# First MLP block split by step, first inverse in 16x16 blocks, and a new early order in a delta-rule attention and MLP kernel

## The chip, the cores and the metric

The kernel runs on one core of a Trainium2 chip. The metric is the device time of one execution in microseconds, shown as the median of several runs. Everything is float32, except that the MLP weights arrive as 8-byte floats and are converted on the chip.

## The reference

There are 4 batches, 8 heads, 768 tokens and 48 values per head. Attention is a delta rule whose state (48x48 per head and batch) is read and changed at every token; the outputs are laid side by side to rows of 384 and go through an MLP with a hard-swish.

```python
k_n = k / (np.linalg.norm(k, axis=-1, keepdims=True) + 1e-06)
for t in range(S):
    y[:, :, t] = einsum('bhd,bhde->bhe', q[:, :, t], state)
    v_old = einsum('bhde,bhd->bhe', state, k_n[:, :, t])
    state = state + beta[t] * outer(k_n[:, :, t], v[t] - v_old)
...
h = x @ w_in                        # (3072, 384) @ (384, 2048)
g = h * clip(h + 3, 0, 6) / 6
out = g @ w_out                     # (3072, 2048) @ (2048, 384)
```

## The kernel before

The 768 tokens are cut into 24 steps of 32 tokens; the four batches stand beside each other on the 128 partitions. Within a step the recurrence is solved by a triangular system: a strictly triangular 32x32 matrix per head and batch (the L part of the tile LB) is inverted, and the inverse X takes L's place. Two steps make an MLP block of 256 columns, so there are 12 blocks.

*Loads.* `load_k`, `load_q` and `load_v` bring one step each in four DMAs of 48 KB. `load_w` brings one of 16 weight pieces (8 of w_in, 8 of w_out, 768 KB each) as raw 8-byte words to a place that is free at the time. SP issues most of them; ACT issues every other early k step, one q step, beta and the first stores of L.

*Weights.* A piece is turned to float32 by `scales` on ACT, which makes the power of two from the exponent bits by five activations (L298), and by `convert` on DVE with three operations (L317, L322, L327), the last of which needs the scale.

*Steps.* `norms` makes the inverse lengths of k for a group of steps (group 0: steps 0 and 1; then groups of four). `prep` multiplies them onto k (kb, POOL L383), makes a mask times beta (mb, L391), transposes kb and qb on PE (pt, L409) with a copy to KQ on ACT (L412), multiplies them (sc, L425), masks the result into LB (DVE L434), makes beta times kb (bkb, L438), and stores L to DRAM for the later groups (L450).

*Inverses.* For steps 0 and 1 `product` inverts by six matrix products on PE (pi, L485), each between DVE transposes and additions; the result is written at L543. For a group of four steps `inverse` loads all 128 triangles of the group, one to a partition, and eliminates with 60 DVE operations (L566 and L571); the result goes through DRAM (L576) back into LB (L584).

*Chain.* `chain` is the recurrence of a step: state times k and q (ks, L622), R (L635), X times R (pz, L643) copied to Z on ACT, the update of the state (su, L710, and L726), the output (py, L643), and the transposed output xT (yt, L699, L700). It needs the state of the step before.

*MLP.* `up` works through the 16 chunks of a block: three matmuls into ph (L760), a ReLU to t on ACT (L765), and the product g on DVE (L772), which is held back in `pending`. It starts when both steps of the block have their xT. `down` multiplies g by w_out (po, L795). From block 2 on, `down_by_seven` does that with seven products of quarters (L856) and sums on DVE (L842).

*Order.* Each engine works in the order in which the program issues. Up to step 5 of the chain that order is a written list of words, `ORDER`, one per piece of work: p, h, i, n, x with a step or group, and a, c, q, v, w, u, g for scales, conversions, loads, MLP chunks and held-back products. After that a loop with a fixed plan of 15 places per step mixes the chain of step t, the prep of a later step, the inverse of the next group and one MLP chunk per place.

Of the kernel before, what the change touches and what calls it, by code (L numbers as in the profile page):

```python
# [22 lines left out]
n0*8 n1 p0 n1 p0 n1 p0 q*2 p0 q p1 q p1 n1 p0 p1 a n1 a*2 p0 q*2 a*2 c a q p1 x0 n1*2 a n1*3 a  # L23
p2*2 x0 q c k2 p2 a p1 p3 x1 c p3*2 p2 a x1*2 p2 p4 p1 a*2 x1 k2*2 p3 p2 a*3 p3 k2 p5 x0 c*2
k2*3 p3 x0 c a*4 x0 k2 c*3 p4 p5 k2*2 x1 k2 x0 p4 c*2 p5 p4 p5 p4*2 p5 x1*2 k2 x0 p5 a x1 a i1 c
x0 x1 a x0 c x1 k2 x1 x0*2 k2 c i1 v k2 i1 x1 i1 x0 i1*2 a i1*2 x0 q i1*3 a i1 h0*2 i1*3 q i1*3
h0 i1*3 v i1 x1 i1 q i1 h0 i1*3 a i1*2 a h1 a*2 h1 i1*2 h0 i1 h1 q h1 i1 c i1 v h1*2 v i1 h1 k2
i1*5 v i1 v i1 v c w v i1 a c a*2 i1 a i1 c i1 v q i1 a v*2 i1 v a c i1*4 w i1*2 h1 n2 i1*4 a
i1*3 a i1 h2 i1*2 c a i1 a i1 n2 a c*2 u a g c n2 a c u a n2 g u n2*3 a n2 q c a g n2*2 a c a p6
h2 u h2 c p6 a w p6 u q*2 a v g q*2 a h2 p6 c q*2 v u p7 a q p6 a q p7 p6 v p8 c g q h2 v h2 a c  # L30
w a p7 a k3 h3 u k3 p8 u a h2*2 k3 c g k3 g c h3 c h3 p8 a u k3 a k3 p7 u g q p8 u q w k3 p7 h3
a p9 p8 c a p9 k4 g p9 k4 p7 a*2 g u k3 k4 c k4 h3 a h3 p9 c w k3 k4 k3 a p9 g*2 h3 a c h4 k4 k3
u a h3 c g k4 h4 k3 c w u p8 k3*2 g k3 h4 k3 q a n3 a c n3 c a n3 u q u g u h4 a g p9 a c k4 h4
c a n3 a u a w k4 i2 w*2 a*2 u n3 a h4 v h5 h4 c a u c g n3 c n3*2 g v*2 u h4 n3 u v n3 u c p10
q a*2 q g k4 v q i2 p11 k4 u k4*4 p10 i2*2 q*2 i2*2 k4 u v i2*2 h5 v g h5 i2 a i2 q i2 p10 u h5
u v i2*2 q u i2*2 c i2 p10 g u i2 p10 i2*4 p11 p10 h5*2 q u q h5 p11 g u p11 i2 u i2*2 p12 i2 g
i2*2 p11*2 u i2*2 u i2*3 g i2 u*2 g i2 u*2 g u g u*2 g u i2*6 u*4 h5
# [4 lines left out]
def kernel(  # L42
# [90 lines left out]
    def load_k(t, eng=nc.sync):  # L133

        g, i = group(t)
        if i == 0:
            needs(*(("kb", first(g - 2) + j) for j in range(size(g - 2) if g >= 2 else 0)))
            kfs[g] = stage.tile([P, GS, H, D], FP32, name="kf", bufs=2)
        for b in range(B):
            eng.dma_start(out=kfs[g][rows(b), i], in_=tokens(k, b, t))  # L140
            if b == B - 1:
                past.add(("k", t))
            yield

    def load_q(t, eng=nc.sync):
        if t < N:
            if t >= NQB:
                needs(("qT", t - NQB))
            for b in range(B):
# [30 lines left out]
    for t in kbufs + qbufs + bkbufs:  # L180
        nc.vector.memset(t[:, :, D:DP], 0.0)

# [5 lines left out]
    for j, value in enumerate((1.0, -1.0)):  # L188
# [10 lines left out]
    nc.vector.tensor_reduce(  # L199
        out=eye[:], in_=ident[:].rearrange("p (b c) -> p c b", b=B), axis=AX.X, op=ALU.add  # L200
    )
    blocks = const.tile([P, C // G], FP32, name="blocks")
    nc.vector.tensor_reduce(
        out=blocks[:], in_=eye[:].rearrange("p (n c) -> p n c", c=G), axis=AX.X, op=ALU.add
    )

    parity = const.tile([P, 2, 2], FP32, name="parity")
    nc.vector.memset(parity[:], 0.0)
    for b in range(B):
        for j, value in enumerate((-1.0, 1.0)):  # L210
            nc.vector.memset(parity[rows(b), b % 2, j : j + 1], value)

    beta_tok = persist.tile([P, N, C], FP32, name="beta_tok")
    nc.vector.transpose(out=beta_tok[:].rearrange("p n h -> p (n h)"), in_=beta_hm)

    state = persist.tile([128, B, NP, D], FP32, name="state")
    nc.vector.memset(state[:], 0.0)
# [11 lines left out]
    for i, value in enumerate((1152 - 7.5 / 16, -1600.0, -448.0, -704.0, 704.0 * 128, 1e-30)):  # L229
        nc.vector.memset(places[:, i : i + 1], value)  # L230
    powers = (
        (ACTF.Relu, 1.0 / 16), (ACTF.Abs, 1.0), (ACTF.Relu, 1.0), (ACTF.Abs, 1.0),
        (ACTF.Relu, -128.0),
    )
    WP, WF = 256, 2
# [9 lines left out]
    raws, parts = {}, {}  # L245


    NR = 4
    ds = [0]
    assert WP * NKT == WF * DM and NR * 2 <= NWI <= 2 * NR and NR * 2 * WF * DM <= NFC * DM  # L250

    def load_w(i, pool=stage):
        if i >= NW:
            return
        dst, src = weights[i]
        if i >= NWI:
            needs(("w", i - NWI + NR - 2 if i < NWI + 2 else i - 2))
        if src.dtype == FP32:
            nc.sync.dma_start(out=dst, in_=src)
            return  # L260
        if NR <= i < NWI:
            n = (i - NR) * 2 * WF
            raw = w_out[:, n : n + 2 * WF, :].rearrange("p f m -> p (f m)").bitcast(U32)
            raws[i] = raw.rearrange("p (s f z) -> p s f z", s=dst.shape[1], z=2)
        else:
            shape = [128, dst.shape[1], dst.shape[2], 2]
            if pool is stage:
                raw = spare[:, ds[0] % 2].bitcast(U32)
                raws[i] = raw.rearrange("p (s f z) -> p s f z", s=shape[1], z=2)
                ds[0] += 1  # L270
            else:
                raws[i] = pool.tile(shape, U32, name="d")[:]
# [15 lines left out]
    def scales():  # L288

        for i in range(NW):  # L290
# [6 lines left out]
            for n, (func, scale) in enumerate(powers):  # L297
# [3 lines left out]
                )  # L301
                if n == len(powers) - 1:
# [3 lines left out]
    def convert():  # L306

        for i in range(NW):
# [803 lines left out]
```

## Time and profile before

| | |
|---|---|
| median of 3 runs | 726.7 us (723.8 to 729.11) |
| span of the profiled execution | 725.1 us |
| busy: PE, DVE, ACT, POOL | 656.7, 454.9, 247.3, 89.5 us |
| first ph matmul of block 0 | 87.60 us |
| first po matmul of block 0 | 148.14 us |
| last matmul ends | 721.3 us |

A busy engine is one with an instruction at work. PE shows every float32 matmul as two records. TensorE's granted clock is shown beside the busy shares. An idle time is named after what ended it.

### The profile page before, as it was taken

How to read it: one execution, taken by the hardware profiler on the slowest of the kernel's cores; microseconds unless marked ns; L12 is line 12 of the kernel's file. 1: busy time of each engine (PE TensorE's matmuls, PEld its weight loads, DVE VectorE, ACT ScalarE, POOL GpSimd, SP SyncE). 2: the span in 40 equal slices, each digit the busy share in tenths (PEclk: the TensorE clock that was granted, in tenths of full speed). 3: DMA queues.
4: the chain of work that ended last, by engine and by line, in shares of the span. 5: the costliest groups of instructions: out<-in, count | busy, mean ns of one | idle time of the engine just before them, and what ended most of it. 6: DMA issues, size and time to landing. Idle time of an engine off the chain costs nothing.

```text
span 725.1 us, 25019 instructions
## 1 busy us (share of the span) xinstructions
PE 656.7 (91%) x10984; PEld 571.9 (79%) x10984; DVE 454.9 (63%) x1209; ACT 247.3 (34%) x467; POOL 89.5 (12%) x128
## 2 busy tenths in 40 slices
PE   0666839798979999999999999999999999999997
PEld 0455627666756789889889899898898898989997
DVE  6556996488583379665489464598444894533343
ACT  1763688593130331331322322322313213222130
POOL 3640024004031101041110031000000000000000
PEclk9966569899999999999999999999999999999999
DMA  7954437472042312421410411212302001000000
GB/s 135 298 119 89 112 91 176 90 183 37 8 96 48 75 32 42 90 36 26 96 32 15 98 33 31 52 21 60 53 2 50 13 16 39 2 24 1 23 1 22
DMA packets 135853, 44.72 MB, mean 62 GB/s; under 512 B 126112, under 2 KB 129184, under 8 KB 135744
## 3 DMA queue, kind: packets, MB, share of 16 engines
q1 hardware_dynamic: 126832, 40.99, 25.4%
q10 hardware_dynamic: 8912, 2.13, 1.5%
q8 instruction: 86, 1.41, 0.8%
q14 instruction: 23, 0.19, 0.1%
HBM read 32.60 MB, written 10.49 MB: 59 GB/s over the span
## 4 chain that ended last, share of the span: by engine, by line
PE 78%; issue 7%; DVE 5%; DMA 4%; POOL 2%; ACT 2%; SPq 1%; POOLq 0%; DVEq 0%
PE ph L760 31%; PE po L856 26%; PE po L795 3%; PE pz L643 3%; PE ks L622 3%; PE su L710 3%; PE py L643 3%; PE pt L409 3%; PE sc L425 2%; DMA kf<-in_k_dram 2%; DMA spare<-in_moe_w_in_dram 1%; PE pi L485 1%; ACT spare L298 1%; DMA vf<-in_v_dram 1%; PE yt L699 1%
## 5 line engine op out<-in xcount | busy, mean ns | idle before, releaser
L760 PE MATMUL ph<-xT,w_in 128*128 128x256 f32 x1152 | 269.6, 386 | 2.6 <-issue 2.3
L760 PEld LDWEIGHTS ph<-xT,w_in 128*128 128x128 f32 x1152 | 216.4, 193 | 34.7 <-issue 3.0
L765 ACT ACTIVATE t<-ph,halves 128x256 f32<-128x256 f32 x192 | 90.8, 474 | 207.3 <-PE ph L760 204.6
L772 DVE SCALAR_TENSOR_TENSOR g<-t,ph 128x256 f32<-128x256 f32 x192 | 79.8, 418 | 120.5 <-ACT t L765 120.3
L856 PE MATMUL po<-w_out,g 128*128 128x192 f32 x640 | 111.9, 327 | 0.0
L856 PEld LDWEIGHTS po<-w_out,g 128*128 128x128 f32 x640 | 104.2, 190 | 0.5
L856 PE MATMUL po<-spare,g 128*128 128x192 f32 x480 | 87.2, 330 | 0.0
L856 PEld LDWEIGHTS po<-spare,g 128*128 128x128 f32 x480 | 78.0, 190 | 1.2
L298 ACT ACTIVATE spare<-spare,places 128x768 uint16<-128x768 uint16 (+1 forms) x74 | 69.2, 940 | 7.7 <-DVE w_in L327 3.3
L566 DVE TENSOR_TENSOR pr<-A 128x30 f32<-128x30 f32 (+19 forms) x180 | 62.8, 349 | 4.1
L571 DVE TENSOR_TENSOR A<-A,pr 128x30 f32<-128x30 f32 (+19 forms) x180 | 61.9, 344 | 4.1
L842 DVE TENSOR_TENSOR g<-g 128x256 f32<-128x256 f32 x160 | 60.4, 428 | 3.7 <-PE po L856 3.5
L409 PE MATMUL pt<-ident,kb 128*128 128x128 f32 x96 | 18.3, 326 | 32.8 <-POOL kb L383 32.8
L795 PE MATMUL po<-w_out,g 128*128 128x384 f32 x128 | 45.4, 494 | 0.0
L383 POOL TENSOR_TENSOR kb<-kf,inv 128x384 f32<-128x384 f32 x24 | 23.5, 979 | 176.0 <-DVE inv L369 73.0
L412 ACT ACTIVATE KQ<-pt 128x512 f32<-128x512 f32 x48 | 28.2, 594 | 47.4 <-PE pt L409 47.4
L409 PEld LDWEIGHTS pt<-ident,kb 128*128 128x128 f32 x96 | 13.8, 167 | 36.0 <-POOL kb L383 33.8
L863 ACT ACTIVATE o<-po 128x192 f32<-128x192 f32 x40 | 13.2, 331 | 82.8 <-PE po L856 79.7
L391 POOL TENSOR_TENSOR mb<-beta_tok,mask 128x256 f32<-128x256 f32 x48 | 33.8, 724 | 56.2 <-DVE LB L434 56.2
L726 DVE TENSOR_TENSOR state<-state,su 128x384 f32<-128x384 f32 x46 | 23.3, 548 | 22.2 <-PE su L710 22.2
L795 PEld LDWEIGHTS po<-w_out,g 128*128 128x128 f32 x128 | 23.5, 192 | 12.9 <-issue 0.5
L635 DVE SCALAR_TENSOR_TENSOR R<-ks,parity,vf 128x192 f32<-128x192 f32 x46 | 16.9, 410 | 26.3 <-PE ks L622 26.2
(97 smaller groups left out, 581.5 us busy)
## 6 DMA issues: line engine op xcount, KB each, us to landing
spare<-in_moe_w_out_dram SPq DMA_DIRECT2D x8, 768.0 KB, 5.4
vf<-in_v_dram SPq DMA_DIRECT2D x96, 48.0 KB, 2.6
qb<-in_q_dram SPq DMA_DIRECT2D x92, 48.0 KB, 2.4
out_dram<-o SPq DMA_DIRECT2D x92, 48.0 KB, 1.6
kf<-in_k_dram SPq DMA_DIRECT2D x84, 48.0 KB, 2.8
w_out<-in_moe_w_in_dram SPq DMA_DIRECT2D x4, 768.0 KB, 9.6
LB<-x_dram SPq DMA_DIRECT2D x22, 128.0 KB, 3.1
x_dram<-A SPq DMA_DIRECT2D x5, 512.0 KB, 2.8
```

The lines of the kernel that those rows point to most:

```text
L298: nc.scalar.activation(out=z, in_=z if n else d.bitcast(I16)[:, :, :, 3], func=func, bias=places[:, n : n + 1], scale=scale,)
L391: nc.gpsimd.tensor_tensor(out=mb[:, e], in0=beta_tok[:, t, e:H:2].unsqueeze(2).unsqueeze(3).to_broadcast([P, NP, 2, C]), in1=mask2[:].unsq ...
L409: nc.tensor.transpose(pt[:, p, :], src[:, 2 * p : 2 * p + 2].rearrange("p e w -> p (e w)"), ident[:])
L566: nc.vector.tensor_tensor(out=pv, in0=A[:, j, j + 1 :].unsqueeze(1).to_broadcast([n, j, w]), in1=A[:, 0:j, j].unsqueeze(2).to_broadcast([n ...
L571: nc.vector.tensor_tensor(out=A[:, 0:j, j + 1 :], in0=A[:, 0:j, j + 1 :], in1=pv, op=ALU.subtract)
L643: nc.tensor.matmul(ps[rows(place(b)), D * h : D * h + D], lhsT=m(h)[rows(b)], rhs=z[rows(b), D * h : D * h + D], start=True, stop=True, sk ...
L760: nc.tensor.matmul(ph[:], lhsT=w_in[:, s, f * 128 : (f + 1) * 128], rhs=xT[:, s, :], start=(s == 0), stop=(s == NKT - 1),)
L765: nc.scalar.activation(out=t1[:], in_=ph[:], func=ACTF.Relu, bias=half, scale=1.0 / 6.0)
L772: nc.vector.scalar_tensor_tensor(out=g, in0=t1[:], scalar=1.0, in1=ph[:], op0=ALU.min, op1=ALU.mult)
L795: nc.tensor.matmul(pos[c][:], lhsT=gs[blk, f // 2][:, f % 2, c * P : (c + 1) * P], rhs=w_out[:, f, :], start=(f == 0), stop=(f == NFC - 1),)
L842: nc.vector.tensor_tensor(out=A(f, *out), in0=A(f, *a), in1=A(f, *b), op=op)
L856: nc.tensor.matmul(ps[n][:], lhsT=A(f - f % 2, *a)[:, f % 2], rhs=b[:, f], start=(f == 0), stop=(f == HF - 1),)
```

## The change

1. *First block by step.* `up(0)` becomes two generators, `up(0, 0)` and `up(0, 1)`, each for the 128 columns of one step, so the first needs the xT of step 0 alone. Each matmul, ReLU and product of block 0 is issued twice with half the columns. ReLUs (`relus`) and products (`pending`) are now both held back, and are words of their own.
2. *First group's inverse.* For group 1 `halves_of` eliminates only the two 16x16 blocks on the diagonal, both in one operation (28 operations instead of 60). `join` then makes the block between them, per step, with two products on PE, two DVE transposes, an addition and a copy on ACT.
3. *Powers of two* take four activations instead of five.
4. *Order.* `ORDER` is new and finer: loads, settings, pads, masks, stores of L, and the output half of a chain are words too, and a piece of work is cut at more places. All loads and stores of L and X are issued by SP. The weights' raw places change, and the temporary pool of the products is replaced by buffers of KQ. Norms of steps 0 and 1 are made one by one, those of group 1 by two; their squares are on ACT, and they take one operation less.

The loop after the list keeps its plan. The diff, cut to its core:

```diff
 ORDER = """
-n0*8 n1 p0 n1 p0 n1 p0 q*2 p0 q p1 q p1 n1 p0 p1 a n1 a*2 p0 q*2 a*2 c a q p1 x0 n1*2 a n1*3 a
...
+k*3 z*2 k w z k z q z*2 q*2 m0 n0 q n0 k n0 m1 k n0*2 k a n0 s k n0 c s k a w c a k p0 q n1 q s p0
+a q*2 p0*2 k c s k p0 s p0 k a q s q p0 a s q x0 m2 a q*2 a q s n1 x0 q s q c n2 b0 q n1 q c q k
...
     powers = (
-        (ACTF.Relu, 1.0 / 16), (ACTF.Abs, 1.0), (ACTF.Relu, 1.0), (ACTF.Abs, 1.0),
-        (ACTF.Relu, -128.0),
+        (ACTF.Relu, 1.0 / 16, 1152 - 7.5 / 16), (ACTF.Abs, 1.0, -1600.0), (ACTF.Abs, 1.0, -1152.0),
+        (ACTF.Relu, -128.0, 704.0 * 128),
     )
...
+    homes = [spare[:, i] for i in range(2)] + [
+        w_out[:, n : n + 2 * WF, :].rearrange("p f m -> p (f m)") for n in range(0, NFC, 2 * WF)
+    ]
+    for i, n in enumerate((0, 1, 2, 3, 4, 5, 0, 1, 3, 4, 5, 0, 1, 5, 0, 1)):
...
-            if g in (2, 3):
+            if g < 4:
                 nc.scalar.activation(out=sq[:], in_=kf[:, i0 + i], func=ACTF.Square)
...
+    def lower(t, dma=nc.sync):
...
+            dma.dma_start(
+                out=l_dram[g][i].rearrange("h p c -> p h c"),
+                in_=LBs[t][:].rearrange("p e a j w -> p (e a) j w")[:, :, 0, :],
+            )
...
+    def join(t):
...
+        nc.vector.transpose(out=T, in_=LT)
+        yield
+        ps = times("pi1", T, HC)
+        yield
+        nc.vector.tensor_tensor(
+            out=S[:, :, HC:C], in0=ps[:], in1=corner[:].unsqueeze(1).to_broadcast([P, H, HC]),
+            op=ALU.add,
+        )
+        nc.vector.transpose(
+            out=T2.rearrange("p h c -> p (h c)"), in_=S.rearrange("p h c -> p (h c)")
+        )
+        yield
+        ps = times("pi2", T2, C)
+        yield
+        nc.scalar.activation(out=LT[:, :, HC:C], in_=ps[:], func=ACTF.Copy)
...
+    def halves_of(g):
...
+        for j in range(1, HC - 1):
+            w = HC - 1 - j
+            nc.vector.tensor_tensor(
+                out=pv, in0=D2[:, :, j, j + 1 : HC].unsqueeze(2).to_broadcast([n, 2, j, w]),
+                in1=D2[:, :, 0:j, j].unsqueeze(3).to_broadcast([n, 2, j, w]), op=ALU.mult,
+            )
+            nc.vector.tensor_tensor(
+                out=D2[:, :, 0:j, j + 1 : HC], in0=D2[:, :, 0:j, j + 1 : HC], in1=pv,
+                op=ALU.subtract,
+            )
...
-    def up(blk):
+    def up(blk, half_of=None):
+        cols = slice(0, TB) if half_of is None else slice(half_of * P, half_of * P + P)
+        name = "u" if half_of is None else "ab"[half_of]
-        needs(*(("seam", blk * CB + i) for i in range(CB)))
+        needs(*(("seam", blk * CB + i) for i in range(CB) if half_of in (None, i)))
...
                 nc.tensor.matmul(
-                    ph[:], lhsT=w_in[:, s, f * 128 : (f + 1) * 128], rhs=xT[:, s, :],
+                    ph[:, cols], lhsT=w_in[:, s, f * 128 : (f + 1) * 128], rhs=xT[:, s, cols],
...
+        ua=up(0, 0), ub=up(0, 1), u=mlp_units(),
...
-            for t in range(LA):
-                drain(load_k(t, nc.scalar if t % 2 else nc.sync))
```

## The prediction

> **What bounds the kernel now.** I read the page's busy shares, then the slices, then busy time by stage, then the timeline at the borders between stages.
>
> ```profile
> PE 656.7 (91%) x10984; PEld 571.9 (79%) x10984; DVE 454.9 (63%) x1209; ACT 247.3 (34%) x467; POOL 89.5 (12%) x128
> ...
> PE   0666839798979999999999999999999999999997
> ...
> PEclk9966569899999999999999999999999999999999
> DMA  7954437472042312421410411212302001000000
> ```
>
> The 91% is an average over two regimes: about 12 slices (18.1 us each) with holes and a reduced clock, then 28 at 9. I therefore cut the span at three events: the first matmul of the first MLP block (ph, 87.6), the first of its down projection (po, 148.1), and the end of step 7's py (250.7). Columns: window, its length, busy us (instructions) of PE, PEld, DVE, ACT, POOL, then granted clock, DMA share, GB/s.
>
> ```profile
> 0.00:87.60 87.60, 47.55 (x1719) 40.18 (x1719) 59.48 (x156) 43.79 (x61) 24.55 (x46) 0.77 0.64 156
> 87.60:148.10 60.50, 43.07 (x906) 36.00 (x903) 43.28 (x96) 43.35 (x68) 13.53 (x16) 0.82 0.52 123
> 148.10:250.70 102.60, 95.59 (x1512) 68.42 (x1511) 65.60 (x157) 35.38 (x64) 21.91 (x28) 0.97 0.32 67
> 250.70:721.30 470.60, 470.51 (x6861) 427.30 (x6853) 286.17 (x802) 124.83 (x276) 29.54 (x39) 1.00 0.17 35
> ```
>
> From 250.7 on PE is idle for 0.1 of 470.6 us. What can be won lies before. The events that hold it there, in the timeline (start, length, engine, line, what; in brackets the idle time before):
>
> ```profile
> 8.89 4.76 ACTq L140 DMA_DIRECT2D kf<-in_k_dram  x8
> 9.11 0.55 DVE L351 TENSOR_REDUCE ss<-sq 128x8 f32<-128x384 f32 x1
> 13.70 0.31 ACT L355 ACTIVATE root<-ss,places 128x16 f32<-128x16 f32 x1 [11.39 <-DMA kf<-in_k_dram]
> ...
> 67.80 0.41 DVE L543 SCALAR_TENSOR_TENSOR LB<-VY,pi 128x256 f32<-128x256 f32 x1
> ...
> 96.54 0.35 SPq L576 DMA_DIRECT2D x_dram<-A  x1
> ...
> 106.25 1.11 PE L409 MATMUL pt<-ident,kb 128*128 128x128 f32 x4 [12.56 <-POOL kb L383]
> ```
>
> Four readings. The first square root could run at 9.7 (ss done) but stands behind ACT's own DMA issues until 13.7. The first step's inverse is ready only at 68.2. The first group's inverse ends at 96.5. PE then waits 12.6 us for a kb that needs norms queued on DVE in between.
>
> [...] clock 0.77 in the first window, and six ph records take 2.16 us at 108.0 against a pitch of 1.29 later. [...] 0 to 38 us is DMA-full (8 or 9 tenths, 130 to 180 GB/s with 48 KB loads, 350 to 400 with weights) with two issuers.
>
> **The change part by part.** I add up PE work at the pitch of the dense stretch (start to start): ph 128x256 matmul 0.43 us, po of 384 columns 0.645, of 192 columns 0.325, ks 1.08 per step, pz, py, sc 0.8, su 0.82, yt 0.33, four pt 0.46; products of the inverse (pi) 0.8, with two operands 1.1. Over the listed instructions this is 613.3 us before; 460.1 of it lies after 250.7 and took 470.6, a factor 1.023.
>
> New PE work: four joins of two pi each, 8 x 0.75 = 6.0; the first block in two halves, 96 matmuls of 128 columns instead of 48 of 256. The trace has none of this form. At half the columns it costs 0.215, at no gain from fewer columns 0.43 (+20.6 in all). I take 0.225, since four pt with a 128x128 weight load each keep 0.44 to 0.46 us, so weight loads do not bind at 0.11. That is +1.0. Total 620.3: +7.0. The part after 250.7 is the same work in both, so the question is when the changed kernel has done 620.3 - 460.1 = 160.2.
>
> *To the first ph.* Work 24.9 on PE (28.8 before; step 1's chain is no longer ahead of it). Three queues run beside it.
> - DMA: all loads now go out on SP. The last v load of step 0 stands behind some 58 loads of 48 KB (0.34 us each: 140 GB/s) and 8 weight pieces (2.0 us each: 385 GB/s), so 2 + 20 + 16 = 38, and 41 landed. It also stands behind the store of step 3's LB (about 37).
> - DVE: to the first state update 45.5 us (conversions 19.4: 8 pieces of 0.55 + 0.95 + 0.96 less the last step; the two products 10.8; LB 4.1; ss 3.8; norms 3.6; settings and state the rest). It starts at 0.9 and idles about 9.6 early, until the first sc: k0 at 4.9, root 8.9 (no DMA issue ahead), kb 11, KQ 13, LB 16.8. End 56; ks1 to 57.
> - ACT: to the first xT 35 power operations x 0.94 = 32.9 (with the old five per piece 41), KQ 12 x 0.595 = 7.1, squares 7 x 0.52 = 3.6, six small copies and Z, y, xT 3.0, roots 1.2: 47.8. From 4.9, with 3.2 waiting for the first ss and some 3 for weight piece 2 (issued 46th on SP): 59.
> So the first ph comes at 59 (87.6 before).
>
> *First half* (16 chunks, steps 1's chain between): PE 10.8 + 3.85 = 14.7. DVE: 26 paired inverse operations of 28 to 112 elements 6.9 (between 0.18 and 0.27 in rows of 30 and 108), 16 g of 128 columns x 0.30 (between 0.18 and 0.418), state, y 2.3: 14.1. ACT 16 x 0.36 + 6 x 0.94 + 0.5 = 11.9. PE and DVE nearly equal, each handing to the other through four banks[...]: 18, to 77. The old inverse was 60 operations (66.1 to 96.5); the new has 28 and ends here at about 75.
>
> *Second half and joins*: PE 10.8 + 3.0 + 3.5 = 17.3; DVE 21.1 (g 4.8, conversions 6.9, R and y of two steps 4.2, ss, state, four join operations); ACT 14. DVE binds, and the join of step 2 waits for the return of the inverse through DRAM (about 84): 23, to 100.
>
> *To work 160.2*: 103.2 left, x 1.023 = 105.6. ACT still owes 19 power operations (17.9 of 25 us beside 23 us of PE work), from which the first po pieces come; the same stretch before had 102.6 for 87.9 x 1.023 = 90, so 12.6 of stalls. I take 10: to 216.
>
> Sum: 216 stands against 250.7, so 725.1 - 34.7 = 690.4. The profiled 725.1 lies 1.6 below the median 726.7 (723.8 to 729.1), so I say 692.
>
> Costed at nothing: settings moved to DVE in pieces and pads on POOL (POOL has 56 us idle before mb); shorter norms (four small operations of 0.18 to 0.35 instead of five; off the path after the first); SP's 21 extra issues (452 for 431, after 60 us SP is the idlest queue); copies split from their matmuls, deferred evictions (ACT 34% busy); the order after 250.7, where blocks stand half a period differently against the steps (ks now at the end of up instead of inside down), hidden while DVE stays near its 61%; if not, half a us a block, 5 in all.
>
> **The rivals.**
> A, the stalls stay: the start comes at 59 but the rest keeps the 35.9 us that stretch lost before (250.7 - 87.6 - 124.3 x 1.023). For: DVE and ACT carry about the same work into a shorter time, and half-size evictions are two for one. Against: the inverse no longer fills DVE. 59 + 135.3 x 1.023 + 35.9 = 233.3, + 474.4 + 1.6 = 709.
> B, denser: first ph at 53 (weights land without waiting), 6 of stalls: 197.4 + 474.4 (250.7 to the end) = 671.8, so 673 against the runs.
> C, slower: SP is the only load queue, and in-order. The store of LB(3) stands before v of step 0, and w_out loads before k and v, each waiting for ACT and DVE readers. If one such reader is late because of data queued behind that wait, the start slides one for one. Slower by over 1% (734) needs work 160.2 done only after 258, 42 us later than I put it, that is v of step 0 landing after 83 instead of 41; at 90 the time is 741. Against: LB(3) needs only loads that stand ahead of it.
> D, nothing won: C with v near 75 (692 + 34 = 726), or A with halves bound by weight loads (709 + 19.6 = 729).
>
> **How the numbers follow.** Main case 0.57 (679 to 704); A 0.22 (704 to 717); B 0.13 (664 to 679); D 0.04; C 0.04. Leaving out the thin ends of B and A: 668 to 714. One per cent, 7.3 us, is about what a measurement here can tell from no change: faster 0.92, same 0.04, slower 0.04.
>
> **What would show it.** First LB of the product before 35 (67.8 before), first ph 55 to 62, end of the inverse 73 to 80, first po 97 to 105, step 7's chain no later than about 225, then PE idle near nothing for some 470 us. Wrong: ph matmuls of 128 columns at a pitch over 0.3; a PE hole over 5 us between 60 and 200; v of step 0 after 50; holes after 250 that the kernel before does not have.

## The result, and the profile after

The changed kernel takes 717.17 us (median of 4 runs, 716.01 to 720.65) beside 725.28 for the kernel before in the same session (723.80 to 729.11): ratio 0.9896, 95% interval 0.9853 to 0.9940. Timed a second time it gave 0.9892 (0.9860 to 0.9925). It is faster by about 8 us where 34 were predicted, and 717.2 lies above the predicted range. The profiled span fell from 725.1 to 714.6.

The page's busy shares, slices and the row of the instruction queue, of the changed kernel:

```profile
PE 657.3 (92%) x11592; PEld 576.5 (81%) x11592; DVE 437.9 (61%) x1187; ACT 241.2 (34%) x479; POOL 88.3 (12%) x145
...
PE   1566978999996999999999999999999999999997
...
PEclk9985898999997999999999999999999999999999
DMA  7677774143116112343014043012051020100000
...
q8 instruction: 91, 1.49, 0.9%
```

DMA is still at 6 or 7 tenths for the first 100 us. The last row will matter: 91 packets of 16 KB on the queue that the page calls "instruction", beside 2 x 11592 instructions of the PE (matmuls and weight loads), so 254.8 for each packet. The kernel before has 86 packets for 2 x 10984, 255.4 for each. Counted in blocks of 256 that is 90.6 and 85.8 blocks.

Busy time by stage, cut at the same events as before: first ph, first po, the point where 160.1 us of PE work are done (counted with the prediction's pitches, so that the same 460 us are left as after 250.7 before), end of the last matmul. Columns as in the prediction: window, length, busy us (instructions) of PE, PEld, DVE, ACT, POOL, clock, DMA share, GB/s.

```profile
0.00:74.95 74.95, 38.49 (x1460) 32.81 (x1460) 46.20 (x104) 44.86 (x67) 27.73 (x65) 0.83 0.74 178
74.95:118.49 43.54, 37.02 (x966) 34.86 (x964) 30.81 (x99) 28.08 (x58) 0.41 (x2) 0.90 0.65 137
118.49:240.10 121.61, 111.05 (x2017) 81.25 (x2013) 75.94 (x179) 43.62 (x79) 28.62 (x36) 0.96 0.33 65
240.10:710.80 470.70, 470.70 (x7160) 427.63 (x7158) 284.60 (x805) 124.68 (x278) 31.56 (x42) 1.00 0.19 37
```

The last stage is as predicted (470.7 for 470.6). The miss lies in the stages before it, against the prediction's own terms:

| stage | predicted | measured | difference |
|---|---|---|---|
| to the first ph | 59 | 74.95 | +16.0 |
| first ph to first po (18 + 23) | 41 | 43.54 | +2.5 |
| first po to work 160 | 116 | 121.61 | +5.6 |
| sum | 216 | 240.1 | +24.1 |

What filled them shows in the list of the PE's waits up to 125 us (line, releaser, us in total, times, longest):

```profile
PE sc L497 <- issue: 6.3, 3, 2.3
PE pi L547 <- issue: 6.1, 4, 3.4
...
PE pi L635 <- issue: 1.9, 1, 1.9
PE pi L635 <- DVE VY L645: 1.9, 1, 1.9
...
PE pz L797 <- issue: 1.5, 1, 1.5
...
PE py L797 <- issue: 1.2, 1, 1.2
```

"issue" means that the PE waited for nothing that the profile shows. There are 12.4 us of it ahead of the first ph and 20 in the whole execution; the kernel before has 5 and 9. In the timeline these stops have a pattern (start, length, engine, line, what; in brackets the idle time before):

```profile
34.95 0.31 PE L497 MATMUL sc<-KQ 64*32 64x64 f32 x7 [0.33 <-ACT KQ L484]
37.38 0.80 PE L497 MATMUL sc<-KQ 64*32 64x64 f32 x57 [2.12 <-issue]
...
39.56 0.79 PE L497 MATMUL sc<-KQ 64*32 64x64 f32 x57
42.62 0.31 PE L497 MATMUL sc<-KQ 64*32 64x64 f32 x7 [2.26 <-issue]
...
58.34 0.59 PE L547 MATMUL pi<-VY 32*32 32x32 f32 x27 [3.38 <-issue]
```

Stops fall into the middle of one step's 64 score records, two for each of its 32 matmuls (the first after 7 of them, the second after 57), where a wait for data would be odd; `shift` below tests that. From one stop to the next I counted 125 to 128 matmul records, or twice that; with their weight loads, 128 records are a block of 256 instructions. Ahead of each of these resumptions the trace has one 16 KB packet of the instruction queue, started 2.3 to 2.8 us before it. Below, a *crossing* is the moment when the PE goes from one block into the next, and a *stop* is an idle time named "issue" at a crossing.

### The profile page after: what moved, and what is told of

It is laid out like the page before. It is cut to its first block, busy times and chain, and to the rows that moved or that the text cites. A ratio compares the mean times of both kernels' runs of the same rounds, so it can differ in the third digit from the quotient of the medians.

```text
span 714.6 us, 26278 instructions
## 1 busy us (share of the span) xinstructions
PE 657.3 (92%) x11592; PEld 576.5 (81%) x11592; DVE 437.9 (61%) x1187; ACT 241.2 (34%) x479; POOL 88.3 (12%) x145
## 4 chain that ended last, share of the span: by engine, by line
PE 84%; issue 8%; DMA 3%; SPq 3%; DVE 1%; ACT 1%; POOL 0%; POOLq 0%; DVEq 0%; ACTq 0%
PE ph L945 36%; PE po L1051 26%; PE po L986 3%; PE ks L776 3%; PE pz L797 3%; PE pt L479 3%; PE su L891 2%; PE py L797 2%; PE sc L497 2%; SPq L148 2%; DMA spare<-in_moe_w_in_dram 1%; PE pi L547 1%; PE yt L840 1%; SPq L160 1%; DMA w_out<-in_moe_w_in_dram 1%
## 5 line engine op out<-in xcount | busy, mean ns | idle before, releaser
L945 PE MATMUL ph<-xT,w_in 128*128 128x256 f32 (+1 forms) x1248 | 272.8, 373 | 6.3 <-DVE g L957 5.7
L945 PEld LDWEIGHTS ph<-xT,w_in 128*128 128x128 f32 x1248 | 221.8, 195 | 35.7 <-DVE g L957 6.5
L954 ACT ACTIVATE t<-ph,halves 128x256 f32<-128x256 f32 (+1 forms) x208 | 94.5, 456 | 244.6 <-PE ph L945 240.1
L957 DVE SCALAR_TENSOR_TENSOR g<-t,ph 128x256 f32<-128x256 f32 (+1 forms) x208 | 82.1, 397 | 104.2 <-ACT t L954 103.6
L720 DVE TENSOR_TENSOR pr<-A 128x30 f32<-128x30 f32 (+19 forms) x150 | 51.7, 345 | 5.7 <-DMA A<-l_dram 2.5
L338 ACT ACTIVATE spare<-spare,places 128x768 uint16<-128x768 uint16 (+1 forms) x56 | 52.3, 940 | 0.9
L725 DVE TENSOR_TENSOR A<-A,pr 128x30 f32<-128x30 f32 (+19 forms) x150 | 50.1, 334 | 3.6
L789 DVE SCALAR_TENSOR_TENSOR y<-ks,parity,y 128x192 f32<-128x192 f32 x46 | 17.0, 413 | 31.1 <-ACT y L813 31.1
L497 PE MATMUL sc<-KQ 64*32 64x64 f32 x1536 | 21.8, 230 | 10.4 <-issue 9.1
L776 PEld LDWEIGHTS ks<-state,KQ 64*64 64x64 f32 x1472 | 24.7, 138 | 7.6 <-issue 5.5
```

What stands on the lines that cost most here:

```text
L338: nc.scalar.activation(out=z, in_=z if n else d.bitcast(I16)[:, :, :, 3], func=func, bias=places[:, n : n + 1], scale=scale,)
L497: nc.tensor.matmul(scv[rows(b), e, p], lhsT=kq[:, 3 if b % 2 else 0, :], rhs=kq[:, 3:1:-1, :] if b % 2 else kq[:, 0:2, :], start=True, sto ...
L720: nc.vector.tensor_tensor(out=pv, in0=A[:, j, j + 1 :].unsqueeze(1).to_broadcast([n, j, w]), in1=A[:, 0:j, j].unsqueeze(2).to_broadcast([n ...
L725: nc.vector.tensor_tensor(out=A[:, 0:j, j + 1 :], in0=A[:, 0:j, j + 1 :], in1=pv, op=ALU.subtract)
L776: nc.tensor.matmul(ph[y][c, e, D * p : D * p + D], lhsT=KQ[r, p * B // 2 + b // 2, 2 * y : 2 * y + 2, :].rearrange("k y c -> k (y c)"), rh ...
L945: nc.tensor.matmul(ph[:, cols], lhsT=w_in[:, s, f * 128 : (f + 1) * 128], rhs=xT[:, s, cols], start=(s == 0), stop=(s == NKT - 1),)
```

## The experiments

Theory "fetch": streams of tiny matmuls use up blocks of instructions faster than these arrive. Its rivals: SP, held by the weight pieces, brings data late; or DVE and ACT, working through the written order, set the pace. Six kernels ran in one execution each: `shift`, `calm`, and the four that leave out part of the work (`thin`, `thin_trip`, `w_third`, `all_three`).

**Is it the block, or these matmuls?** `shift` moves every later PE instruction by 64 records:

```diff
-        for p in range(NP):
+        for p in [*range(NP)] * (2 if t == 0 else 1):
```

> The changed kernel with the 32 score matmuls of step 0 written twice over (the second writes the same values), so that all later instructions of the PE stand 64 instructions further on in its program. Fetch theory: the PE's idle stretches that the trace calls issue sit at instruction-block boundaries, every 256 PE instructions (128 matmuls with their weight loads), so counted in the program as it was they move 32 matmuls earlier, while the count of matmuls before each stays a multiple of 128 plus the same remainder: the first six stay at the same remainder, at other matmuls. If instead those stretches are waits of these particular matmuls for data or a semaphore that the trace doesn't show, each stays at its old matmul, 32 records later in the count. The time: within 4 us of the changed kernel either way.

The stops stayed at the count and left the matmuls. Matmul records issued at each stop of over 0.25 us ahead of the first ph:

```
changed kernel  475  601  726  980 1108 1236 1363
shift           475  601  728  980 1108 1236 1364 1491
```

In the timeline of `shift` the first stop is now inside a product of step 0, the second among the transposes:

```profile
34.74 0.26 PE L547 MATMUL pi<-VY 32*32 32x32 f32 x7
36.48 0.69 PE L547 MATMUL pi<-VY 32*32 32x32 f32 x57 [1.48 <-issue]
...
38.38 0.27 PE L479 MATMUL pt<-ident,kb 128*128 128x128 f32 x1
42.70 1.65 PE L479 MATMUL pt<-ident,kb 128*128 128x128 f32 x7 [4.05 <-issue]
```

So they are block ends, and no waits of these matmuls for data. (The one execution took 713.3 us; `shift64` below is the same program, timed.)

**Does it need a full DMA?** `calm` writes step 14's scores nine times over, at 282 us:

```diff
-        for p in range(NP):
+        for p in [*range(NP)] * (9 if t == 14 else 1):
```

> The changed kernel with the score matmuls of step 14 (at 282 us, where the DMA engines are about three tenths busy) written nine times over instead of once: 512 more matmul records, four blocks of 256 PE instructions, same values, same output. It measures how fast the PE can be fed with tiny matmuls when DMA is calm. Fetch with a floor of its own: the stream runs at its own pitch of 1.6 to 2.2 us per 128 records only for the first block, then stands at each block's end; a block lasts 3.5 to 3.9 us, the gaps are 1.3 to 2.2 us each, and the 512 records take 13 to 15.5 us. If only a full DMA makes the fetch late: no gap over 0.3 us and 6.5 to 9 us in all.

The PE's timeline there:

```profile
283.52 1.20 PE L497 MATMUL sc<-KQ 64*32 64x64 f32 x101
286.36 1.47 PE L497 MATMUL sc<-KQ 64*32 64x64 f32 x128 [1.63 <-issue]
290.09 1.92 PE L497 MATMUL sc<-KQ 64*32 64x64 f32 x128 [2.26 <-issue]
294.09 2.04 PE L497 MATMUL sc<-KQ 64*32 64x64 f32 x128 [2.08 <-issue]
297.82 1.57 PE L497 MATMUL sc<-KQ 64*32 64x64 f32 x91 [1.69 <-issue]
```

128 records need 1.5 to 2.0 us (1.5 at a granted clock of 1.00, 1.9 to 2.0 at 0.50 to 0.55), and a block comes only every 3.73, 4.00 and 3.73. After each of the first three resumptions the next packet of the instruction queue started 1.1 us later, and each packet started 2.4 to 2.9 us ahead of the resumption that it led to, while the DMA engines went from 0.51 busy to 0.02. So a full DMA is not needed for the stops: about 3.7 us per block remain with DMA nearly idle. The shortest time from one stop to the next in any of the runs is 3.5 us (`w_third`).

**Fewer instructions.** `thin` halves the matmuls of the first two steps' products:

```diff
-            for h in range(H):
+            for h in range(0, H, 2):
...
-                        ps[rows(b), 0:n, w], lhsT=T[rows(b), w], rhs=rhs[rows(b), :, w],
+                        ps[rows(b), 0:n, ww], lhsT=T[rows(b), w], rhs=rhs[rows(b), :, ww],
```

> The changed kernel with half the matmuls in the products that invert the first two steps: 16 of twice the columns in place of 32 in each call, every second head's left factor left out (a pair of heads shares one), so the output is not the reference's; DMA, DVE and ACT do the same as in the changed kernel. PE instructions ahead of the first up-projection fall from 1395 matmul records to about 1010. Fetch (a block of 256 PE instructions lasts at least 3.6 us, because its successor's transfer starts 1.1 us or more after the crossing and the PE goes on 2.3 to 2.9 us after that start): the gaps ahead of the first up-projection fall from 12.4 us to 7 or less, and it comes at 66 to 71 instead of 75. Rival, that DMA load alone holds the start: gaps as long each, only fewer, and data late all the same, first up-projection within 2 us of 75. Rival, DVE and ACT order: within 2 us of 75 as well.

The matmul records ahead of the first ph fell from 1459 to 1075 (the expectation's two counts are too low by 64). Stops fell from 12.4 to 6.4 us, and the first ph came at 69.85; `thin_trip`, the same up to there, has 69.26, and the five executions of kernels that equal the changed one up to there lie between 74.95 and 79.85. Not all of that is the stops: the PE's busy time ahead of the first ph fell too, from 38.5 to 34.4 us, and its waits for DVE grew from 8.2 to 12.0. But the first po came at 120.2, and the one execution took 718.6: the gain was gone 50 us later. The timeline of `thin` between:

```profile
83.69 0.09 DVE L693 MEMSET A<- 128x32 f32 x1
...
90.05 0.39 SPq L695 DMA_DIRECT2D x_dram<-A  x1
94.46 2.43 SPq L702 DMA_DIRECT2D LB<-x_dram  x4
97.69 0.45 DVE L646 STREAM_TRANSPOSE VY<-LB 128x256 f32<-128x256 f32 x1 [5.49 <-DMA LB<-x_dram]
98.19 1.05 PE L636 MATMUL pi<-LB,VY 16*32 16x16 f32 x64 [5.16 <-DVE VY L646]
```

The elimination ends at 83.7 (87.7 in the changed kernel), but SP comes to its store only at 90.05, behind k and v loads (90.29 there), so the first join starts about when it did there (98.2 and 98.9). Behind the first bound stands a second.

**The second bound.** `trip` and `thin_trip` issue the inverse's way back on the POOL queue, alone and on top of `thin`:

```diff
-        nc.sync.dma_start(
+        nc.gpsimd.dma_start(
             out=x_dram[g][:].rearrange("t h (b c) i -> (t h b) (c i)", b=B), in_=A,
...
-            nc.sync.dma_start(out=LBv[:, :, 0, :], in_=x_dram[g][i]
+            nc.gpsimd.dma_start(out=LBv[:, :, 0, :], in_=x_dram[g][i]
```

> The changed kernel with the first group's inverse going back to DRAM and the four loads of its halves issued on the POOL queue instead of SP's (POOL has three operations of 0.2 us between 60 and 100 us). Theory of two bounds: in the changed kernel the elimination ends at 87.7, its store is issued at 90.3 behind 14 loads on SP, its first load at 95.1 behind 7 more, and the first join's product starts at 98.9 after a PE hole of 1.9 us; with the trip on POOL the store goes out at 87.8, the first half lands by 94 and the hole ahead of the first join goes: first output-projection 2 to 4 us earlier than 118.5, whole 1 to 4 us faster than the changed kernel (ratio to before 0.984 to 0.989). If the PE and DVE bind that stretch all the same: under 1 us.

> Half the matmuls in the first two steps' products, as in the run named thin (every second head's left factor left out), and the inverse's way back on the POOL queue, as in trip. Thin alone brought the first up-projection 5.1 us earlier (69.85) but the first output-projection came at 120.2, with a PE hole of 5.2 us ahead of the first join, where DVE waited 5.5 us for the first loaded half: the elimination ended at 83.7 there and its store was issued on SP only at 90.1. Two bounds, one behind the other: with both out of the way the hole ahead of the join is under 1 us and the first output-projection comes at 111 to 115. If the start's gain is lost to something else: it comes at 118 or later.

`trip` was a miss: ratio 0.9914 (0.9880 to 0.9947), no gain over the changed kernel. In its profile the hole ahead of the join is gone, but its start came at 79.3 with 17.3 us of stops, and from there to the first po it took 42.9 us (43.5 in the changed kernel). Nor is the missing hole its doing for certain: in the second execution of the changed kernel (`after_again` below), whose start came as late, the hole is 0.2 us with the trip on SP. `thin_trip` was right: first po at 113.2, 710.6 us for the one execution. Its timeline:

```profile
83.12 0.09 DVE L693 MEMSET A<- 128x32 f32 x1
83.51 0.73 POOL L695 DMA_DIRECT2D x_dram<-A  x1 [27.45 <-PE ph L946]
87.35 3.54 POOL L702 DMA_DIRECT2D LB<-x_dram  x4 [0.37 <-DMA x_dram<-A]
91.55 0.44 DVE L646 STREAM_TRANSPOSE VY<-LB 128x256 f32<-128x256 f32 x1
```

DVE has no wait for the half any more. Removing either bound alone brought nothing at the first po (118.5 in the changed kernel, 120.2 in `thin`, 122.2 in `trip`); with both removed it came 5 us earlier, in one execution.

**Bytes, and who issues them.** `w_third` transfers the first of the slices of each weight piece alone; `w_pool` leaves the bytes and takes the first six pieces off SP:

```diff
-            out=raws[i].rearrange("p s f z -> p s (f z)"), in_=src.bitcast(U32)
+            out=raws[i].rearrange("p s f z -> p s (f z)")[:, 0:1], in_=src.bitcast(U32)[:, 0:1]
```

```diff
-        nc.sync.dma_start(
+        (nc.gpsimd if i < 6 else nc.sync).dma_start(
             out=raws[i].rearrange("p s f z -> p s (f z)"), in_=src.bitcast(U32)
```

> The changed kernel, but each weight piece transfers a third (the first matrix) or half (the second) of its bytes, and the conversion reads that slice in place of the others: what it leaves out is the other slices of the weights, so the output is not the reference's. Number of transfers, conversions and matmuls are as in the changed kernel. Three theories of why the first up-projection matmul came at 74.95 us and not at 59. Fetch (the PE stands still at every 128th matmul record because the next block of instructions comes late while the DMA engines are full; 12.4 us of such gaps before the first up-projection): with the bytes of four early pieces down to a third the gaps shrink to under 6 us and the first up-projection comes at 62 to 68. Held SP (each 768 KB piece holds SP about 5 us, and the k, q, v and lower-triangle transfers behind it come late): SP's waits on the pieces fall from 5 us to under 2, the first product's lower triangle lands by 31 instead of 36, v of step 0 by 46 instead of 53, and the first up-projection comes at 65 to 70 with the gaps still there. Order (DVE and ACT do the written order one after the other, DMA is beside the point): within 2 us of 74.95.

> The changed kernel with the first six weight pieces issued on the POOL queue instead of SP's; same bytes, same order of the words. Held SP: SP no longer stands 5 us behind each piece, k and the lower triangles of step 0 come 3 to 6 us earlier, v of step 0 lands by 46 instead of 53, and the first up-projection comes at 66 to 70, the whole at 708 to 712. Fetch: the same bytes fill the same engines, the issue gaps of the PE before the first up-projection stay at 10 to 14 us, and the whole is within 3 us of the changed kernel. A cost that speaks against: POOL itself is held by the pieces (5 us each), and its k scaling and masks come late; then the first up-projection is later than 75 and the whole slower by 3 to 8 us.

`w_third`: first ph at 66.77, stops 5.2 us, first po at 108.4, one execution 706.0. `w_pool`: first ph at 77.09, stops 15.1, ratio 0.9897 (0.9870 to 0.9923), nothing won; the last v load of step 0 went out at 50.4 there, no earlier than in the changed kernel (50.8), where SP's longest wait for a piece up to 90 us is 3.0 us and not the 5 of the expectation (from issue to landing the pieces took 4.4 to 9.1 us in the median, by place). In these runs the bytes count, not the queue that issues them. Both theories had called for an earlier ph in `w_third`; its SP also came sooner to its loads (the load of the lower triangles for the elimination went out at 61.4, not 69.7), so it doesn't part the two; `w_pool` and `shift` do. Where bytes seem to matter to the fetch is before the packet starts. With DMA quiet it starts 1.1 us after the crossing (`calm`); in the changed kernel it starts 4.2 us after the crossing at 42.62, where weights flow and the DMA engines are 0.88 busy. From its start to the resumption it is 2.2 to 3.2 us in every stop of over 0.6 us, in all runs.

**All together.**

> The three cuts together: half the matmuls in the first two steps' products (every second head's left factor left out), a third or a half of each weight piece's bytes (the other slices left out), and the inverse's way back on the POOL queue. If instruction blocks and weight bytes are all that held the start, first up-projection at 59 to 63 and first output-projection at 99 to 104, the prediction's numbers, and the whole at 694 to 702. If a third bound (the order on DVE and ACT) stands behind them: first up-projection at 64 to 66, hardly earlier than the 66.8 that fewer bytes gave alone.

The edit is the sum of `thin`, `trip` and `w_third`. The first ph came at 64.82 with 1.8 us of stops, the first po at 108.7, one execution 707.0: neither 59 nor 100. The third bound that the expectation named is there. The PE around its start:

```profile
62.56 2.32 PE L777 MATMUL ks<-state,KQ 64*64 64x48 f32 x64 [2.79 <-DVE state L907]
64.82 6.82 PE L946 MATMUL ph<-xT,w_in 128*128 128x128 f32 x48
```

and the queues that it waits for:

```profile
59.81 0.49 ACT L845 ACTIVATE xT<-yt 128x384 f32<-128x384 f32 x1 [0.27 <-PE yt L841]
...
61.54 0.41 DVE L608 SCALAR_TENSOR_TENSOR LB<-VY,pi 128x256 f32<-128x256 f32 x1
61.87 1.01 DVE L907 TENSOR_TENSOR state<-state,su 128x384 f32<-128x384 f32 x2
```

xT of step 0 is ready at 60.3, what the prediction called 59. The ph stands behind ks of step 1 in the PE's order, ks behind the state on DVE, the state behind the last result of step 1's product: 4.5 us more. An order without that was not tried.

One subtraction sums this up. First ph less the stops ahead of it is 62.6 in the changed kernel, 63.5 in `thin`, 61.6 in `w_third`, 63.0 in `all_three`, and lies between 60.2 and 66.3 in all 17 profiled executions of kernels whose first block is halved; the stops themselves go from 1.8 to 17.3 us. This is bookkeeping, and no proof that the stops alone set the start: no run took them away and left all else as it was.

**The parts.** `five` undoes part 3, `before_four` makes it alone in the kernel before, `whole_block` undoes part 1, `whole_inverse` part 2. Their core:

```diff
-        (ACTF.Relu, 1.0 / 16, 1152 - 7.5 / 16), (ACTF.Abs, 1.0, -1600.0), (ACTF.Abs, 1.0, -1152.0),
-        (ACTF.Relu, -128.0, 704.0 * 128),
+        (ACTF.Relu, 1.0 / 16, 1152 - 7.5 / 16), (ACTF.Abs, 1.0, -1600.0), (ACTF.Relu, 1.0, -448.0),
+        (ACTF.Abs, 1.0, -704.0), (ACTF.Relu, -128.0, 704.0 * 128),
...
-        ua=up(0, 0), ub=up(0, 1), u=mlp_units(),
+        ua=up(0, 0), ub=up(0, None, "b"), u=mlp_units(),
...
-            ("i", g), lambda: halves_of(g) if g == 1 else inverse(g, nc.sync, nc.sync), g < NG
+            ("i", g), lambda: paced() if g == 1 else inverse(g, nc.sync, nc.sync), g < NG
...
-        "n": early_norms, "m": mask, "b": scaled, "l": lower, "x": lambda t: product(t) if t < CB else join(t),
+        "n": early_norms, "m": mask, "b": scaled, "l": lower, "x": lambda t: product(t) if t < CB else iter(()),
```

> The changed kernel with part three undone: five ACT operations per power of two instead of four, so 14 more of 0.94 us (13 us of ACT), some 7 of them ahead of the first up-projection. If ACT's sum sets the start, as the prediction had it: the first up-projection comes 6 to 8 us later and the whole is 7 to 12 us slower than the changed kernel, ratio to before 0.999 to 1.006. If instruction fetch and data set the start: the first up-projection moves by less than 3 us, the first output-projection by 2 to 6, the whole is 2 to 5 us slower, ratio 0.992 to 0.997.

> The kernel before with part three alone: four ACT operations per power of two, the pieces in their old places (13 us less of ACT in all). If ACT's sum is part of what bounds the early stretch of the kernel before, as part three gave 5 us in the changed kernel (five against changed): 2 to 6 us faster than before, ratio 0.992 to 0.997. If in the old order other queues bind (the chain of step 1 and the elimination on DVE): within 1.5 us, ratio 0.998 to 1.002.

> The changed kernel with part one undone: the up-projection of the first block in one piece of 256 columns, in the places of the second half; nothing of it runs beside the chain of step 1 and the short elimination. The 10.8 us of PE work of the first half no longer lie at 75 to 91, but the chain of step 1 and the elimination go on without it and end some 5 to 8 us earlier. Expected by the prediction's sum: 5 to 10 us slower than the changed kernel, ratio 0.996 to 1.004. Fetch rival: 48 fewer up-projection matmuls are 0.4 of a block, no difference from that; without the half block between them the tiny matmuls of step 1 and of the joins stand closer together and the issue gaps after 75 grow from 8 to 10 or more, 8 to 14 us slower.

> The changed kernel with part two undone: the first group's inverse eliminated whole, 60 DVE operations, paced two or three to a place of the 28, and no joins (8 products of 32 matmuls, 512 matmul records, leave the PE's stream). By the prediction's sum: DVE has about 10 us more at 75 to 91, so the elimination ends at 96 to 100 instead of 88, against 4 us of joins saved: 4 to 8 us slower, ratio 0.995 to 1.001. Fetch theory: the joins are four blocks of PE instructions that stand in gaps at 101 to 118 (4.6 us of them), and these gaps go too, so the loss is smaller or none: ratio 0.985 to 0.993.

| kernel | ratio to before | interval | first ph | first po |
|---|---|---|---|---|
| changed | 0.9896 | 0.9853 to 0.9940 | 74.95 | 118.5 |
| `five` | 0.9965 | 0.9946 to 0.9983 | 76.00 | 120.7 |
| `before_four` | 0.9959 | 0.9939 to 0.9979 | 87.4 | 147.1 |
| `whole_block` | 0.9954 | 0.9927 to 0.9980 | 91.63 | 125.1 |
| `whole_inverse` | 0.9894 | 0.9868 to 0.9920 | 74.41 | 118.5 |

Part 3 is worth 0.7% (some 5 us) in the changed kernel and 0.4% (3 us) alone. The first ph of `five` comes 1 us later, inside the changed kernel's own spread, so ACT's sum does not set the start as the prediction had it; the loss shows after it. Part 1 is worth about 0.6%, 4 us, just under what the prediction's sum gave; the 8 to 14 us of the fetch rival did not come. Part 2 is worth nothing that these runs can tell, as the fetch theory had it: without it the elimination ends at 99.9 instead of 87.7, but the eight products of the joins (512 records, four blocks) are gone, total stops fall from 20 to 16 us, and the first po comes at the same 118.5. The losses without part 1 and without part 3 add up to about the whole gain, within their intervals; they were not undone together, and the order alone was not tried against the old one.

**Smaller ones.** `sq_act` takes the squares of group 4 to ACT (`if g < 4` becomes `if g < 5`). `early_trip` has `trip` and step 1's words earlier in the list:

```diff
-... n1 q c q k
-x0 k*2 n2 x0 k x0 k c x0 k*2 n2 x0 k*2 n1 x0 n2 k n1 n2 v n1*2 n4 x0 p1 w*2 n4 x0 b1 w n2 w n2 p1
+... n1 q c n1*2 q k
+x0 k*2 n1*2 p1 n2 x0 k x0 k c x0 p1 k*2 n2 x0 p1 k*2 x0 p1 n2 k n2 p1 v n4 x0 p1 w*2 n4 x0 b1 w n2 w n2 p1
...
```

`after_again` is the changed kernel once more. `shift64`, `shift32` and `shift96` repeat 32, 16 and 48 of step 0's score matmuls.

> The changed kernel with the squares of the fifth group's norms on ACT instead of POOL. In the changed kernel's trace DVE waits three times for a POOL square (0.83 us each) around 220 to 226 us, just ahead of an R and a g of the MLP, and the PE has holes of 5.7 us there. If these waits make the holes: the holes before the up-projection at 220 to 226 shrink from 5.7 to under 3, and the whole is 2.5 to 4 us faster (ratio 0.994 to 0.997). If the holes come from the order of the words around them: under 1 us either way.

> The changed kernel with the words of step 1 earlier in the written order (its norms' last four operations straight after the root, its transposes, scores and lower triangle between the products of step 0, the first three words of its product among the last of step 0's), and the inverse's way back on the POOL queue. The PE then has 136 matmul records ahead of 30 us that stood after it, while its blocks still come faster than they are used. Fetch theory: about one block (3.7 us) leaves the stretch from 35 to 72, the first up-projection comes 2 to 5 us earlier than the changed kernel's (72 in place of 75 to 78), first output-projection at 114 to 118, whole 2 to 5 us faster than after_again. Rival: what holds the end of that stretch is v of step 0 and the last lower triangles, not the PE's blocks, and the step moved only waits elsewhere (DVE and ACT reach its transposes early and stand): within 1.5 us.

> The changed kernel itself once more, for the spread of the start from one execution to the next[...]. First up-projection between 74 and 79, as in the runs whose program is the same up to there (75.0, 77.9, 78.2), gaps before it 10 to 16 us, ratio to before 0.986 to 0.993.

> The same program as the run named shift (step 0's 32 score matmuls twice), timed. If the place of the block ends counts: ratio to before 0.979 to 0.985, and the stretch from the first up-projection to the first output-projection is 38 to 40 us again. If it was chance: 0.987 to 0.993, as the changed kernel.

> Step 0's first 16 score matmuls written twice, so every later PE instruction stands 32 matmul records further on. If the place of the block ends counts, its gaps lie at matmuls halfway between those of the changed kernel and of shift64 and its time differs from one of them by over 3 us. If not: ratio to before 0.987 to 0.993.

> 48 score matmuls of step 0 over again, 96 matmul records further on. If the place of the block ends counts, the time differs from the changed kernel's or from shift64's by over 3 us. If not: ratio to before 0.987 to 0.993.

`sq_act`: 0.9899 (0.9847 to 0.9952), no gain. The hole at 226 in front of six ph changed its name from g (5.7 us) to KQ (4.9 us); the waits for squares were not what made it. `early_trip`: 0.9912 (0.9876 to 0.9948), no gain; the stop at 475 still came, and ahead of the first ph (76.5) the stops (13.5 us) and the PE's waits for DVE (8.5) are much as in the two executions of the changed kernel (12.4 and 14.9; 8.2 and 8.0). `after_again`: first ph at 79.85, above the expected 74 to 79, stops 14.9. One program's start thus moves by 5 us between executions, so a smaller difference between single executions says nothing. `shift64`, `shift32` and `shift96`: 0.9840 (0.9793 to 0.9887), 0.9877 (0.9832 to 0.9923) and 0.9887 (0.9836 to 0.9939). `shift64` repeats the short stretch to the first po (37.9 us again, for 43.5 and 42.7 in the two executions of the changed kernel) and has the lowest median of the kernels timed more than once, with 32 more matmuls; the medians of `shift32` and `shift96` lie 3.4 and 2.7 us above it. Its interval still meets theirs and that of the changed kernel, so whether the place of the block ends is worth 3 us stays open.

## Why the prediction was wrong, by its own steps

- *To the first ph, 59.* This is the step that failed, by +16 us. It says "Three queues run beside" the PE's work, and counts the PE at its pitch. The PE's own supply of instructions was not among the queues: the 1459 matmul records ahead of the first ph are 11 blocks, and after a stop no block came sooner than 3.5 us (`w_third`). Stops take 12.4 us there. That they are block ends is shown by `shift`, that a block takes about 3.7 us even with DMA quiet by `calm`; that the first ph would come earlier by all of the 12.4 is argued from the subtraction above. In `all_three` it came 10.1 us earlier with 10.6 us less of stops. The other 3.6 agree with the order on DVE and the PE (4.5 us in `all_three`), which no run changed.
- *Its DMA term, v of step 0 at 41.* The last load was issued at 50.8 and landed at 53.6, right behind the store of LB(3), as the term had feared; that LB came only at 49.6, behind three stops, and not at about 37. In `all_three`, with few stops and fewer weight bytes, it was still issued right behind that store, at 42.8, and landed at 45.2. The order of the queue was read rightly; the time of LB(3) was not.
- *Its ACT term, 59 to the first xT:* 72.2, but 60.3 in `all_three`. *Its DVE term, 56 to the end of the state:* 62.9 there, 7 too small. DVE is idle for 17.1 of those 64.8 us, 7.6 of them after 18, most of it in round trips between the products and PE or ACT, where the term had no idle time. (The term's 19.4 for the conversions is 18.7 by its own figures, which changes nothing.)
- *First half and joins, 41*: 43.5, with 4.6 us of stops in it. The 128-column ph at 0.225 us was nearly right: 24 records, 12 matmuls, in 2.94 us are 0.245.
- *10 us of stalls to work 160*: 15.6. Stops of 3.3 us and the hole of 5.7 at 226 make up 9; the rest was not taken apart.
- *The part after*: right to 0.1 us.
- *The clock*: 0.83 in the window to the first ph, for 0.77 before. Within it the granted clock is given as 1.00 up to 40 us, the first 13.6 of which the PE stood, and as 0.50 from 60 to 75. What sets it these runs do not show.
- *Costed at nothing*: SP as "the idlest queue" after 60 us. It is not so between 78 and 98, where it holds the inverse's store and loads; this hides the gain of an earlier start (`thin` against `thin_trip`).
- *What stays*: in `all_three` work 160 is done at 230.7. That is 9.4 of the 24.1 us; the other 14.7 (5.8, 2.9 and 6.0 in the three stages) remain there, so what that run takes away (most stops ahead of the first ph, weight bytes, the inverse's way back on SP) is under half of the whole miss. It still has 12.9 us of stops, 6.9 of them between first ph and first po.
- *The signs*: the product's LB came at 36.3 (before 35 asked for), the elimination's end at 87.7 (73 to 80), first po at 118.5 (97 to 105); all were late, as the first ph was. Step 7's py ended at 264.0 (225 asked for, 250.8 before): from there to the last matmul 447 us were left, for 470 before, so the new order puts more work ahead of it, and this sign did not measure what it was to. Of the signs of being wrong one came: v of step 0 landed after 50 (53.6). There was no hole of over 5 us between 60 and 200, and none after 250.
- *The rivals*: A had the stalls stay at 35.9 us behind a start at 59; they came to 165.2 - 135.3 x 1.023 = 26.8, and the start was late. Its range, 704 to 717, ends just below the measured 717.2, but by another way. No case had a start at 75.
- The profile before had the sign: 9.3 us of "issue" on the PE, two of them stops of over 2 us, also in front of a large ph:

```profile
PE pi L485 <- issue: 4.7, 4, 2.7
...
PE ph L760 <- issue: 2.3, 1, 2.3
```

The traces show the block by its count (91 packets of 16 KB; stops 125 to 128 matmul records apart, or twice that) and its cost by where the PE stood. After 250 us, in the changed kernel, the PE has no idle time named "issue": 128 ph records take 27.6 us there (0.216 each), and over all forms the stage from 240.1 on has 7160 records in 470.70 us, 8.4 us for 128. Ahead of that, 20 us of stops stand in the open in this execution.

## What to carry to other kernels

Count the instructions of a stretch as you count its work: here a block of 256 PE instructions came every 3.5 (`w_third`) to 4.0 us (`calm`) at best where the PE stood waiting for it. By an estimate from these two, each over 128, a long stream of matmul records whose own pitch is below some 27 to 31 ns is bound by their number; the records of `calm` ran at 11 to 16 ns (1.47 to 2.04 us for 128) and stood at each of the four crossings. Fewer, larger matmuls brought the first ph earlier here (`thin`, 69.85 for 74.95), an earlier place for step 1 did not (`early_trip`, 76.5); large matmuls put between the tiny ones were not tried. An "issue" idle time that recurs at equal counts of instructions points to that; inserting half a block and seeing whether the stops stay at the count told it from a wait here (`shift`: 475 and 601 in both programs). When the first bound of a stretch is taken away, look at what each queue has in front of the next hand-over before you count the gain: in `thin` the inverse was ready at 83.7, and its store went out at 90.05, behind the loads that stand ahead of it in SP's order.

## What the runs showed of the hardware that I had not expected

- From the start of an instruction packet to the PE's resumption it was 2.2 to 3.2 us in all stops of over 0.6 us, whether the DMA engines were full or idle; the packet alone took 0.9 to 2.0. Its start was 1.1 us after the crossing with DMA quiet (`calm`), 4.2 with weights flowing in the changed kernel, and 6.0 at the longest (`whole_block` at 79.9, DMA 0.99 busy).
- The same DVE conversion (128x768, unsigned to float, L365) took 1.46 us at 12.9, 20.7 and 34.4, while POOL made kb or bkb, and 0.94 to 0.96 at 60, 63, 68 and 71, while POOL did nothing. At 51.1 it took 1.01 although POOL made mb all the while, so a busy POOL alone does not make the 1.46; the cause was not tested.
- In the same program the first ph came at 74.95 and at 79.85 in two executions, and the medians still agree within 0.4%.
